# Attention in groups of 128 tokens and all heads, with q, k and the output transposed by DMA, ahead of a SwiGLU block

## The chip, the cores and the metric

The kernel runs on one core of a Trainium2 chip. The metric is the device time of one execution in microseconds (us), as the median of several runs. The profile comes from one of these executions. Its span, from the first to the last instruction, is about 2 us shorter than the run's time.

The engines are PE (matmul), DVE (vector), ACT (scalar functions), POOL (general purpose) and SP (which here only issues DMAs). In the timelines below, each of them works through its own instructions in order (in the change, ACT's first exp, whose scores PE had finished by 11.7 us, stands behind DMA issues and starts at 28.8 us).

## The reference

```python
q, k, v: (8, 8, 576, 64)            # batch, heads, tokens, head_dim
scores = q @ k.T / 8, masked to 0 <= row - column < 64
attn   = softmax(scores) @ v
x      = attn as (4608, 512)        # tokens, heads * head_dim
out    = (silu(x @ w_gate) * (x @ w_val)) @ w_out     # d_ff = 1536
```

Inputs and output are float32. Both kernels compute in bf16 with float32 sums, write silu by way of tanh, and skip the maximum of the softmax.

## The kernel before

A unit is 512 tokens of one pair of heads; there are 36 (9 blocks of 512 tokens, 4 pairs). q and k come in as float32 on partitions of tokens, are cast on POOL and transposed on PE. The keys of a pair are copied into `kbd`, a block-diagonal tile, so that one matmul serves both heads.

```python
def transposes(u):
    q_b, k_b = ready.pop(u)
    tp = ps_a.tile([P, 2, 512], BF16, name="tp", tag="a")
    for i, x in enumerate((q_b, k_b)):
        for c in range(4):
            nc.tensor.transpose(tp[:, i, P * c:P * c + P], x[:, c, :], identb[:])
    qT = att.tile([P, 512], BF16, name="qT", tag="qT")
    nc.scalar.copy(qT[:], tp[:, 0, :])
    kb = kbd[t % 2]
    kt = tp[:, 1, :].rearrange("r (j x) -> r j x", x=64)
    nc.vector.tensor_copy(kb[0:64, p, :, 0:64], kt[0:64])
    nc.vector.tensor_copy(kb[64:128, p, :, 64:128], kt[64:128])
```

The output comes out with channels on partitions, so the softmax sums must be known on every partition. A matmul with a matrix of ones gives them, and DVE takes the reciprocal of a whole 128x512 tile:

```python
def products(u):
    ...
    for c in range(2):
        nc.tensor.matmul(d_ps[:], bones[:], E[:, :, c, :], start=(c == 0), stop=(c == 1))
    nc.vector.reciprocal(r[:], d_ps[:])
    nc.vector.tensor_mul(xT[t][:, p, :], o_ps[:], r[:])
```

A regular round runs one unit of attention ahead of a quarter of the FFN of an earlier block:

```python
gate_value(t, 3 * s)            # 8 matmuls 128x512, tanh on ACT, two DVE operations
products(w + 4)
gate_value(t, 3 * s + 1)
transposes(w + 5)
project(t - 1, s, ps_o, "o")    # 12 matmuls 128x512, copy on ACT, store
load(w + 8); casts(w + 6); scores(w + 5)
gate_value(t, 3 * s + 2)
```

All DMAs go out from SP, some 20 in a round.

The softmax here doesn't subtract the row's maximum and nothing guards it: scores larger than these inputs give would overflow.

Of the kernel before, what the change touches and what calls it, by code (L numbers as in the profile page):

```python
# [17 lines left out]
def kernel(  # L18
# [14 lines left out]

    nc = tc.nc
# [3 lines left out]
    NU = NT * 4  # L38
# [5 lines left out]
    cast = ctx.enter_context(tc.tile_pool(name="cast", bufs=2))  # L44
# [11 lines left out]
    kbd = [cst.tile([P, 4, 8, P], BF16, name=f"kbd{i}") for i in range(2)]  # L56
    vbd = [cst.tile([P, 4, 8, P], BF16, name=f"vbd{i}") for i in range(2)]
    identb = cst.tile([P, P], BF16, name="identb")
    bones = cst.tile([P, P], BF16, name="bones")
    mask = cst.tile([P, 8, 2, 64], BF16, name="mask")  # L60

    def segments(t):

        n0 = 64 * t
        segs = []
        if n0 > 0:
            segs.append((0, t - 1, S - n0, min(n0, 512)))
        if n0 < 512:
            segs.append((n0, t, 0, 512 - n0))
        return segs  # L70

    staged = {}

    def load(u):
        t, p = divmod(u, 4)
        q_f = stage.tile([P, 4, 2, D], FP32, name="q_f", tag="q_f")
        k_f = stage.tile([P, 4, 2, D], FP32, name="k_f", tag="k_f")
        v_f = stage.tile([P, 8, D], FP32, name="v_f", tag="v_f")
        for dst, src in ((q_f, q), (k_f, k)):
            for off, b, s0, n in segments(t):  # L80
                o, s, left = off, s0, n
                while left:
                    if o % P or left < P:
                        m, r = 64, 64
                    else:
                        m, r = left // P * P, P
                    for a in range(2):
                        nc.sync.dma_start(  # L88
                            dst[o % P:o % P + r, o // P:o // P + max(1, m // P), a, :],
                            src[b, 2 * p + a, s:s + m].rearrange("(c r) d -> r c d", r=r),  # L90
                        )
                    o, s, left = o + m, s + m, left - m
        for off, b, s0, n in segments(t):
            for a in range(2):
                nc.sync.dma_start(
                    v_f[64 * a:64 * a + 64, off // 64:(off + n) // 64],
                    v[b, 2 * p + a, s0:s0 + n].rearrange("(j r) d -> r j d", r=64),
                )
        staged[u] = (q_f, k_f, v_f)

    ready = {}

    def casts(u):
        t, p = divmod(u, 4)
        q_f, k_f, v_f = staged.pop(u)
        q_b = cast.tile([P, 4, P], BF16, name="q_b", tag="q_b")
        k_b = cast.tile([P, 4, P], BF16, name="k_b", tag="k_b")
        nc.gpsimd.tensor_copy(q_b[:], q_f[:].rearrange("r c h d -> r c (h d)"))  # L108
        nc.gpsimd.tensor_copy(k_b[:], k_f[:].rearrange("r c h d -> r c (h d)"))  # L109
        vb = vbd[t % 2]  # L110
        nc.gpsimd.tensor_copy(vb[0:64, p, :, 0:64], v_f[0:64])
        nc.gpsimd.tensor_copy(vb[64:128, p, :, 64:128], v_f[64:128])
        ready[u] = (q_b, k_b)
# [3 lines left out]
    def weights_gv(s):  # L117
        for i, src in enumerate((moe_w_gate, moe_w_val)):
            w_f = wst.tile([P, 4, 384], FP32, name="w_f", tag="w_f")
            nc.sync.dma_start(  # L120
                w_f[:], src[:, 384 * s:384 * s + 384].rearrange("(c r) f -> r c f", r=P)
            )
            raw[i, s] = w_f

    def casts_gv(s):
        for i, dst in enumerate((wg, wv)):
            nc.vector.tensor_copy(dst[:, :, 384 * s:384 * s + 384], raw.pop((i, s))[:])

    def weights_o(s):
        w_f = wst.tile([P, 3, DM], FP32, name="wo_f", tag="w_f")  # L130
        nc.sync.dma_start(
            w_f[:], moe_w_out[384 * s:384 * s + 384].rearrange("(c r) f -> r c f", r=P)
        )
        raw[2, s] = w_f

    def casts_o(s):
        nc.vector.tensor_scalar_mul(wo[:, 3 * s:3 * s + 3, :], raw.pop((2, s))[:], 0.5)

    queries = {}

    def transposes(u):
        t, p = divmod(u, 4)
        q_b, k_b = ready.pop(u)
        tp = ps_a.tile([P, 2, 512], BF16, name="tp", tag="a")
        for i, x in enumerate((q_b, k_b)):
            for c in range(4):
                nc.tensor.transpose(tp[:, i, P * c:P * c + P], x[:, c, :], identb[:])  # L147
        qT = att.tile([P, 512], BF16, name="qT", tag="qT")
        nc.scalar.copy(qT[:], tp[:, 0, :])  # L149
        kb = kbd[t % 2]  # L150
        kt = tp[:, 1, :].rearrange("r (j x) -> r j x", x=64)
        nc.vector.tensor_copy(kb[0:64, p, :, 0:64], kt[0:64])  # L152
        nc.vector.tensor_copy(kb[64:128, p, :, 64:128], kt[64:128])  # L153
        queries[u] = qT

    weights = {}

    def scores(u):
        t, p = divmod(u, 4)
        qT = queries.pop(u)  # L160
        E = att.tile([P, 8, 2, 64], BF16, name="E", tag="E")
        Ef = E[:].rearrange("r m c x -> r (m c x)")
        for h in range(2):
            s_ps = ps_a.tile([P, 512], FP32, name="s_ps", tag="a")
            lo = 0
            if u < 4 and h == 0:
                lo = 64
            else:
                j = 4 * h - 1
                kb = kbd[t % 2][:, p, j, :] if j > 0 else kbd[(t - 1) % 2][:, p, 7, :]  # L170
                nc.tensor.matmul(s_ps[:, 0:64], kb, qT[:, 256 * h:256 * h + 64])
            for i in range(4):
                n = P if i < 3 else 64
                j = 4 * h + i
                nc.tensor.matmul(  # L175
                    s_ps[:, 64 + P * i:64 + P * i + n],
                    kbd[t % 2][:, p, j, :],
                    qT[:, 64 * j:64 * j + n],
                )
            nc.scalar.activation(  # L180
                Ef[:, 512 * h + lo:512 * h + 512], s_ps[:, lo:512], AF.Exp, scale=0.125
            )
            nc.gpsimd.tensor_mul(  # L183
                Ef[:, 512 * h + lo:512 * h + 512],
                Ef[:, 512 * h + lo:512 * h + 512],
                mask[:].rearrange("r m c x -> r (m c x)")[:, lo:512],
            )
            if t < 8 and t // 4 == h:
                nc.gpsimd.memset(E[:, t, 0, :], 0.0)
        weights[u] = E  # L190

    xT = {}

    def products(u):
        t, p = divmod(u, 4)
        E = weights.pop(u)
        Ef = E[:].rearrange("r m c x -> r (m c x)")
        if p == 0:
            xT[t] = xpool.tile([P, 4, 512], BF16, name="xT", tag="xT")
        o_ps = ps_a.tile([P, 512], FP32, name="ao_ps", tag="a")  # L200
        first = True
        for j in range(-1, 8):
            if j < 0 and t == 0:
                continue
            vb = vbd[t % 2][:, p, j, :] if j >= 0 else vbd[(t - 1) % 2][:, p, 7, :]
            lo, hi = max(0, 64 * j), min(512, 64 * j + P)
            e0 = 64 * (2 * j + 1) if j >= 0 else 0
            nc.tensor.matmul(
                o_ps[:, lo:hi], vb, Ef[:, e0:e0 + hi - lo],
                start=first, stop=(j == 7), skip_group_check=True,  # L210
            )
            first = False
        d_ps = ps_a.tile([P, 512], FP32, name="ad_ps", tag="a")
        for c in range(2):
            nc.tensor.matmul(d_ps[:], bones[:], E[:, :, c, :], start=(c == 0), stop=(c == 1))  # L215
        r = att.tile([P, 512], FP32, name="r", tag="r")
        nc.vector.reciprocal(r[:], d_ps[:])  # L217
        nc.vector.tensor_mul(xT[t][:, p, :], o_ps[:], r[:])  # L218
# [3 lines left out]
    def gate_value(t, m):  # L222
# [13 lines left out]
        nc.vector.scalar_tensor_tensor(sg[:], th[:], 1.0, g_ps[:], ALU.add, ALU.mult)  # L236
        nc.vector.tensor_mul(hT[t][:, m, :], sg[:], v_ps[:])  # L237

    def project(t, s, pool, tag):
        o_ps = pool.tile([P, 512], FP32, name="o_ps", tag=tag)  # L240
# [6 lines left out]
        nc.scalar.copy(os_[:], o_ps[:])  # L247
        nc.sync.dma_start(out[512 * t + P * s:512 * t + P * s + P, :], os_[:])


    for u in range(4):
        load(u)
    weights_gv(0)
    load(4)
    for i in range(2):
        nc.vector.memset(kbd[i][:], 0.0)
    make_identity(nc, identb[:])
    for i in range(2):
        nc.vector.memset(vbd[i][:], 0.0)
    casts(0)  # L260
# [111 lines left out]
```

## Time and profile before

| | before |
|---|---|
| time, median of 3 | 470.63 us (470.52 to 470.74) |
| span of the profiled execution | 468.9 us |
| regular round | 11.53 us |
| a round without attention (at the end) | 7.77 us |
| first gate matmul | 40.8 us |
| first gate matmul after 24 gate/value steps and 4 projections | 149.8 us |

The last row is read from the timeline of PE. It is there because the two kernels fill their start-up with different amounts of FFN work: at that point both have done the same. The text calls it the milestone, or the start of the regular rounds.

Lines of the page of the kernel before: busy time of each engine with its share of the span; the strips, which cut the span in 40 slices and give the busy tenths of each (9 is 90% or more); the DMA queue; and the chain of waits that ended last, by engine and by line.

```profile
span 468.9 us, 6826 instructions
PE 367.7 (78%) x2332; PEld 189.3 (40%) x2332; DVE 338.8 (72%) x380; ACT 145.2 (31%) x253; POOL 176.9 (38%) x258
...
PE   1453866738888888888888888888888888889996
...
DMA  7965567741332355333333443233343330001012
...
q1 hardware_dynamic: 129280, 47.22, 39.3%
...
DVE 52%; PE 35%; ACT 4%; SPq 3%; issue 2%; POOL 2%; DMA 1%; DVEq 0%; POOLq 0%; ACTq 0%
```

PE has the most busy time, but the chain names DVE first. The groups say why. Their columns are line, engine, operation, tiles, shapes and count, then the busy time, the mean ns of one, and the idle time of the engine just before them with what ended it:

```profile
L217 DVE RECIPROCAL r<-ad_ps 128x512 f32<-128x512 f32 x36 | 120.7, 3353 | 5.0 <-PE ad_ps L215 5.0
...
L175 PE MATMUL s_ps<-qT,kbd_93 128*128 128x128 bf16 (+1 forms) x160 | 14.0, 232 | 33.0 <-DVE kbd_93 L153 31.6
...
L175 PE MATMUL s_ps<-qT,kbd_94 128*128 128x128 bf16 (+1 forms) x128 | 10.3, 224 | 29.2 <-DVE kbd_94 L153 29.2
```

PE stood idle for 61 us in all before the score matmuls, until DVE had copied the keys. The timeline of DVE in one regular round shows what held the copies. Columns are the start, the length, and then the instruction:

```profile
245.14 3.35 DVE L217 RECIPROCAL r<-ad_ps 128x512 f32<-128x512 f32 x1
248.53 0.69 DVE L218 TENSOR_TENSOR xT<-ao_ps,r 128x512 bf16<-128x512 f32 x1
249.13 0.68 DVE L236 SCALAR_TENSOR_TENSOR sg<-th,g_ps 128x512 f32<-128x512 f32 x1
249.91 0.69 DVE L237 TENSOR_TENSOR hT<-sg,v_ps 128x512 bf16<-128x512 f32 x1
250.52 0.41 DVE L152 COPY kbd_94<-tp 64x512 bf16<-64x512 bf16 x1
250.94 0.43 DVE L153 COPY kbd_94<-tp 64x512 bf16<-64x512 bf16 x1
```

The reciprocal of 3.35 us and what queues up behind it stand ahead of the key copies, and PE gets its scores at 251.42 us after a gap of 1.81 us.

### The profile page before, as it was taken

The numbers are of one execution on the slowest core, as the hardware profiler recorded it, in microseconds if no ns is written. First come the engines' busy times: TensorE is split into PE (matmuls) and PEld (weight loads), VectorE is DVE, ScalarE is ACT, GpSimd is POOL, SyncE is SP. The second block draws the span as 40 slices with busy tenths as digits, with TensorE's granted clock in tenths as the row PEclk, the third lists the DMA queues.
The fourth block names the chain that finished last, engine by engine and source line by source line (L and its number), as shares of the span: only waits on it lengthen the run. The fifth ranks groups of instructions, "written<-read, shape, count | busy, mean of one in ns | idle before, by whom it ended". The sixth has DMA issues, their size and how long they took to land.

```text
span 468.9 us, 6826 instructions
## 1 busy us (share of the span) xinstructions
PE 367.7 (78%) x2332; PEld 189.3 (40%) x2332; DVE 338.8 (72%) x380; ACT 145.2 (31%) x253; POOL 176.9 (38%) x258
## 2 busy tenths in 40 slices
PE   1453866738888888888888888888888888889996
PEld 0331433414444444444444444444444444444443
DVE  7188798777777777777777777777777777776540
ACT  1220222313333333333333333333333333323232
POOL 3873445424444444444444444444444433110000
PEclk9975897879999999999999999999999999999999
DMA  7965567741332355333333443233343330001012
GB/s 173 253 182 130 154 183 209 219 104 46 87 87 67 79 138 124 87 76 82 87 86 92 119 111 90 70 90 92 90 113 92 91 89 24 22 24 45 22 46 89
DMA packets 129314, 47.65 MB, mean 102 GB/s; under 512 B 119040, under 2 KB 123136, under 8 KB 129280
## 3 DMA queue, kind: packets, MB, share of 16 engines
q1 hardware_dynamic: 129280, 47.22, 39.3%
q8 instruction: 18, 0.29, 0.3%
q14 instruction: 16, 0.13, 0.1%
HBM read 37.75 MB, written 9.44 MB: 101 GB/s over the span
## 4 chain that ended last, share of the span: by engine, by line
DVE 52%; PE 35%; ACT 4%; SPq 3%; issue 2%; POOL 2%; DMA 1%; DVEq 0%; POOLq 0%; ACTq 0%
DVE r L217 24%; PE g_ps L229 14%; PE v_ps L229 9%; DVE hT L237 9%; DVE sg L236 8%; PE o_ps L242 6%; DVE xT L218 5%; PE s_ps L175 4%; ACT th L234 3%; SPq L88 2%; POOL E L183 2%; DVE kbd_93 L153 1%; DVE kbd_94 L153 1%; DVE kbd_93 L152 1%; PE ad_ps L215 1%
## 5 line engine op out<-in xcount | busy, mean ns | idle before, releaser
L183 POOL TENSOR_TENSOR E<-E,mask 128x512 bf16<-128x512 bf16 (+1 forms) x72 | 84.5, 1185 | 215.4 <-ACT E L180 215.4
L236 DVE SCALAR_TENSOR_TENSOR sg<-th,g_ps 128x512 f32<-128x512 f32 x108 | 73.9, 684 | 86.5 <-ACT th L234 86.4
L217 DVE RECIPROCAL r<-ad_ps 128x512 f32<-128x512 f32 x36 | 120.7, 3353 | 5.0 <-PE ad_ps L215 5.0
L229 PE MATMUL g_ps<-xT,wg 128*128 128x512 bf16 x432 | 115.4, 391 | 2.9 <-DVE xT L218 2.9
L229 PE MATMUL v_ps<-xT,wv 128*128 128x512 bf16 x432 | 114.3, 388 | 0.0
L234 ACT ACTIVATE th<-g_ps 128x512 f32<-128x512 f32 x108 | 64.5, 597 | 128.4 <-PE g_ps L229 128.4
L242 PE MATMUL o_ps<-wo,hT 128*128 128x512 bf16 x432 | 98.6, 379 | 0.0
L237 DVE TENSOR_TENSOR hT<-sg,v_ps 128x512 bf16<-128x512 f32 x108 | 74.2, 687 | 11.6 <-PE v_ps L229 0.6
L229 PEld LDWEIGHTS <-wv 128*128 128x128 bf16 x432 | 43.3, 100 | 57.2 <-issue 8.6
L180 ACT ACTIVATE E<-s_ps 128x512 bf16<-128x512 f32 (+1 forms) x72 | 39.1, 592 | 68.6 <-PE s_ps L175 68.6
L242 PEld LDWEIGHTS <-hT 128*128 128x128 bf16 x432 | 41.1, 98 | 44.6
L229 PEld LDWEIGHTS <-wg 128*128 128x128 bf16 x432 | 40.9, 100 | 44.5 <-issue 3.5
L175 PE MATMUL s_ps<-qT,kbd_93 128*128 128x128 bf16 (+1 forms) x160 | 14.0, 232 | 33.0 <-DVE kbd_93 L153 31.6
L149 ACT COPY qT<-tp 128x512 bf16<-128x512 bf16 x36 | 21.1, 586 | 45.6 <-PE tp L147 45.6
L175 PE MATMUL s_ps<-qT,kbd_94 128*128 128x128 bf16 (+1 forms) x128 | 10.3, 224 | 29.2 <-DVE kbd_94 L153 29.2
L147 PE MATMUL tp<-identb,q_b 128*128 128x128 bf16 x144 | 14.8, 229 | 16.9 <-POOL q_b L108 16.9
L215 PE MATMUL ad_ps<-E,bones 128*128 128x512 bf16 x72 | 23.1, 405 | 5.4 <-DVE r L217 5.4
L175 PEld LDWEIGHTS <-kbd_93 128*128 128x128 bf16 x160 | 10.8, 107 | 39.1 <-DVE kbd_93 L153 36.3
L218 DVE TENSOR_TENSOR xT<-ao_ps,r 128x512 bf16<-128x512 f32 x36 | 24.9, 692 | 1.2
L108 POOL CAST q_b<-q_f 128x512 bf16<-128x512 f32 x36 | 22.7, 630 | 6.1 <-DMA q_f<-in_q_dram 4.5
L109 POOL CAST k_b<-k_f 128x512 bf16<-128x512 f32 x36 | 22.1, 613 | 4.3 <-PE g_ps L229 3.3
L147 PEld LDWEIGHTS <-q_b 128*128 128x128 bf16 x144 | 11.3, 102 | 26.0 <-POOL q_b L108 18.2
(77 smaller groups left out, 240.7 us busy)
## 6 DMA issues: line engine op xcount, KB each, us to landing
w_f<-in_moe_w_gate_dram SPq DMA_DIRECT2D x4, 768.0 KB, 5.4
w_f<-in_moe_w_val_dram SPq DMA_DIRECT2D x4, 768.0 KB, 7.1
q_f<-in_q_dram SPq DMA_DIRECT2D x32, 96.0 KB, 3.8
k_f<-in_k_dram SPq DMA_DIRECT2D x32, 96.0 KB, 2.4
wo_f<-in_moe_w_out_dram SPq DMA_DIRECT2D x4, 768.0 KB, 6.0
q_f<-in_q_dram SPq DMA_DIRECT2D x16, 128.0 KB, 2.8
k_f<-in_k_dram SPq DMA_DIRECT2D x16, 128.0 KB, 3.2
v_f<-in_v_dram SPq DMA_DIRECT2D x16, 128.0 KB, 3.2
```

What stands on the lines that cost most here:

```text
L147: nc.tensor.transpose(tp[:, i, P * c:P * c + P], x[:, c, :], identb[:])
L175: nc.tensor.matmul(s_ps[:, 64 + P * i:64 + P * i + n], kbd[t % 2][:, p, j, :], qT[:, 64 * j:64 * j + n],)
L180: nc.scalar.activation(Ef[:, 512 * h + lo:512 * h + 512], s_ps[:, lo:512], AF.Exp, scale=0.125)
L183: nc.gpsimd.tensor_mul(Ef[:, 512 * h + lo:512 * h + 512], Ef[:, 512 * h + lo:512 * h + 512], mask[:].rearrange("r m c x -> r (m c x)")[:, ...
L215: nc.tensor.matmul(d_ps[:], bones[:], E[:, :, c, :], start=(c == 0), stop=(c == 1))
L217: nc.vector.reciprocal(r[:], d_ps[:])
L218: nc.vector.tensor_mul(xT[t][:, p, :], o_ps[:], r[:])
L229: nc.tensor.matmul(ps[:], w[:, c, P * m:P * m + P], xT[t][:, c, :], start=(c == 0), stop=(c == 3),)
L234: nc.scalar.activation(th[:], g_ps[:], AF.Tanh, scale=0.5)
L236: nc.vector.scalar_tensor_tensor(sg[:], th[:], 1.0, g_ps[:], ALU.add, ALU.mult)
L237: nc.vector.tensor_mul(hT[t][:, m, :], sg[:], v_ps[:])
L242: nc.tensor.matmul(o_ps[:], hT[t][:, c, P * s:P * s + P], wo[:, c, :], start=(c == 0), stop=(c == 11),)
```

## The change

The intent is to take the large reciprocal and the ones-matmuls away. A unit becomes a group of 128 tokens and all 8 heads. The products are turned round: the tokens are on the output's partitions, the values get two columns of ones (130 columns wide), so that the sums come out of the same matmul as one number per token and head, and the reciprocal has 4 columns. The price is that `x` now has tokens on its partitions and must be transposed for the FFN. That transpose and those of q and k go to DMA, so that PE and the PSUM copies are free of them. q, k and the weights are loaded by few large DMAs issued on ACT; v, the stores and the transposes are issued on SP. The start-up interleaves the first two blocks of 512 tokens.

The core of the diff (the loads, score layout, start-up order and lines within these pieces are cut):

```diff
-        for i, x in enumerate((q_b, k_b)):
-            for c in range(4):
-                nc.tensor.transpose(tp[:, i, P * c:P * c + P], x[:, c, :], identb[:])
-        nc.scalar.copy(qT[:], tp[:, 0, :])
+    def turn(g):
+        sp.dma_start_transpose(out=kT[:], in_=k_b[:])
+        sp.dma_start_transpose(out=qT[:, g % QR], in_=q_b[:])
+    def spread(g):
+        for a in range(2):
+            dve.tensor_copy(
+                kb[64 * a:64 * a + 64, :, :, 64 * a:64 * a + 64],
+                kT[64 * a:64 * a + 64].rearrange("r p (i x) -> r p i x", i=2),
+            )
...
-        for c in range(2):
-            nc.tensor.matmul(d_ps[:], bones[:], E[:, :, c, :], start=(c == 0), stop=(c == 1))
-        nc.vector.reciprocal(r[:], d_ps[:])
-        nc.vector.tensor_mul(xT[t][:, p, :], o_ps[:], r[:])
+            dve.reciprocal(r[:], o_ps[:, :, P:VW])          # 128x4
+            dve.tensor_mul(x_b[...], o_ps[:, :, 0:P]..., r[:]...)
+        sp.dma_start_transpose(out=xT[t][:, :, P * s:P * s + P], in_=x_b[:])
...
+    for w in range(8, NG):
+        turn(w + 6)
+        gate_value(t, 3 * s)
+        products(w + 4)
+        spread(w + 6)
+        casts(w + 7, pool)
+        gate_value(t, 3 * s + 1)
+        scores(w + 6, pool)
+        casts_v(w + 6)
+        load_v(w + 8, sp)
+        load_qk(w + 9, act)
+        project(t - 1, s, ps_o, "o")
+        gate_value(t, 3 * s + 2)
```

## The prediction

> **What bounds it now.** Three stages, read from the chain of waits and the timeline.
> (a) To about 103 us: start-up. The 40-slice strip shows DMA engines 50-90% busy at 130-250 GB/s and PE mostly half idle. Only the 12 gate/value steps of the first 512 tokens get done.
> (b) 103 to 414 us: 27 equal rounds of 11.53 us, each a quarter of 512 tokens. The chain alternates DVE (52%) and PE (35%). In each round DVE's reciprocal (128x512, 3.35 us, 121 us in all) holds back the kbd copies behind it; PE waits 1.8-2.0 us for them before the scores (61 us under "PE s_ps <- DVE kbd" in the waits). PE's own work in a round: FFN 7.77 us (read off the last rounds, which have no attention and repeat every 7.77 us) plus attention, about 1.8 us.
> (c) From 422 us: four rounds of pure FFN and a last projection (10.4 us), PE-bound.
> SP is near its limit too: some 20 DMA issues per round at about 0.55 us each, 11 of 11.5 us.
>
> **Removed.** The big reciprocal: 36 x 3.35 us becomes 72 of 4 columns, about 0.1 us each (estimate from 6.5 ns per column). PE transposes (36 x 8 x 128 columns) and the ones-matmuls for the sums (36 x 2 x 512): 74k columns, 31 us of PE at the traced 0.86 us per 4x512. ACT's qT copy (21 us). kbd copies from PSUM (30 us), replaced by copies from SBUF.
> **Added.** Products stream 3x130 columns per pair: 56k instead of 37k, +8 us PE. PE attention per 128 tokens: 20 matmuls at about 57 ns (traced spacing of the 128-column ones) = 1.15 us. [...] 108 DMA transposes of 128 KB on SP. [...]
> **Moved.** q/k/weight loads to ACT's queue (2-4 issues, 1-2 us per round; ACT then about 5.5 us). Start-up order: 512-token blocks 0 and 1 are interleaved, so PE has 24 gate/value steps and 4 projections to run while weights arrive.
>
> **Sum.** Steady rounds become PE-bound: 7.77 + 1.15 = 8.9, say 9.0 us. First gate at about 40 us, as now (same bytes to load). From there to the regular rounds: 41.5 (24 steps) + 10.4 (projections) + 11 (attention of ten groups) plus some cold clock and waits: they start at about 110 us, with 31 us more FFN done than now at 103. Then 24 x 9.0 = 216, 4 x 7.77 = 31, end 10.4 + 3.5. Span about 371-377; time 378 us, range 355 to 430. Gain: about 60 us from rounds, about 30 from start-up.
>
> Chances: faster 0.88, same 0.05, slower 0.07.
>
> **Signs.** Right if the chain is mostly PE in the middle, with PE 90% busy or more at a period of 8.9-9.3 us; DVE about 60-65%; no reciprocal among the costly groups; the chain names DMA transposes only in start-up. Start-up right if the first gate matmul comes near 40 us and the first projection near 100 us.
>
> **What would make it wrong.** SP occupied over about 2 us per transpose: then SP sets the period (3T + 2.7 us; T = 3 gives 11.7 us, no gain). The same if transposes stall ordinary DMA traffic, or if DVE waits for kT. In start-up, transposes compete with saturated loads, and each group needs three in series; the first gate could slip to 60 us. ACT's in-order DMA issues might delay tanh.

DVE's copies from SBUF (the "spread") had no traced copy behind them, and the sign "DVE about 60-65%" rested on that estimate. The forecast's sum loses no term: it came to a span of about 371 to 377 us and a time of 378 us, range 355 to 430. That SP and DVE keep below PE's 9.0 us in a round, which the sum takes for granted, was an estimate. "Cold clock" in it is the granted clock in the trace of the kernel before: 0.88 in the first 40 us, 0.80 from 40 to 103 us, 1.00 in the rounds. ACT's 5.5 us fit six traced operations of about 0.6 us and the 1 to 2 us of issues.

## The result, and the profile after

The changed kernel takes 452.9 us (451.52 to 453.13, 3 runs) against 470.63 us. The ratio is 0.9615, with a 95% interval of 0.9585 to 0.9645. It is faster, by a fifth of what was predicted (17.7 us against 93), and outside the predicted range. Ratios here are the mean time of one kernel's fast runs over that of the other's fast runs in the same rounds, so they are not quite the ratio of the medians.

The same lines of the page, of the kernel after:

```profile
span 451.1 us, 6021 instructions
PE 347.6 (77%) x2032; PEld 174.5 (39%) x2032; DVE 230.7 (51%) x482; ACT 126.0 (28%) x219; POOL 151.6 (34%) x221
...
PE   0014363755767676999999999999899999999996
...
DMA  9999569965493359678987778976868842110012
...
q1 hardware_dynamic: 103104, 33.06, 38.7%
q10 hardware_dynamic: 80832, 28.32, 29.1%
...
PE 43%; DMA 22%; DVE 17%; POOL 5%; ACT 4%; issue 4%; SPq 2%; ACTq 1%; DVEq 0%; POOLq 0%
```

DVE lost 108 us of work. PE is at 9 in the middle slices where it was at 8. But the first 16 slices (180 us) are poor, with PE mostly at 3 to 7, and DMA is now 22% of the chain. The queues' share of the DMA engines has risen from 39% to 68%. The groups that replace the reciprocal, and the copies of the keys:

```profile
L216 DVE RECIPROCAL r<-ao_ps 128x4 f32<-128x4 f32 x72 | 12.5, 174 | 4.6 <-PE ao_ps L212 4.4
L217 DVE TENSOR_TENSOR x_b<-ao_ps,r 128x256 bf16<-128x256 f32 x72 | 30.5, 424 | 2.5
```

The reciprocals cost 12.5 us where they cost 120.7. In a regular round PE has one small gap left. From the timelines of PE and DVE:

```profile
257.48 0.22 PE L175 MATMUL s_ps<-qT,kbd_93 128*128 128x128 bf16 x1
258.17 0.23 PE L181 MATMUL s_ps<-qT,kbd_94 128*128 128x128 bf16 x1 [0.47 <-DVE kbd_94 L132]
```

```profile
257.19 0.42 DVE L217 TENSOR_TENSOR x_b<-ao_ps,r 128x256 bf16<-128x256 f32 x1
257.54 0.58 DVE L132 COPY kbd_94<-kT 64x512 bf16<-64x512 bf16 x2
```

The key copies follow the normalisation in DVE's order, and here only that order makes them wait: the transposed k had landed at 256.25 us. In 6 of the 22 regular rounds, though, they began within 0.2 us of k's landing, so there the landing was what held them. The period is 9.54 us instead of the 9.0 that was predicted.

Two milestones on PE's timeline divide the time:

| | before | after | predicted |
|---|---|---|---|
| first gate matmul | 40.8 us | 57.6 us | 40 us |
| first gate matmul after 24 gate/value steps and 4 projections | 149.8 us | 173.5 us | 110 us |
| from there to the end of the span | 319.1 us | 277.6 us | 261 us |

So the regular rounds gained 41.5 us and the start-up gave 23.7 us of it back. By this milestone it had been expected to gain 40. The question for the experiments is therefore what holds the start-up.

The waits of the changed kernel in the first 182 us (the line that waited, what it waited for, us in all, how often, the longest):

```profile
PE s_ps L181 <- DVE kbd_94 L132: 21.2, 3, 15.4
PE s_ps L175 <- DMA qT<-q_b: 20.3, 8, 3.9
...
ACT L185 <- DMA v_f<-in_v_dram: 27.5, 1, 27.5
...
ACT th L239 <- DMA kT<-k_b: 19.7, 3, 7.2
...
PE g_ps L234 <- DVE sg L241: 11.8, 3, 4.2
```

Two kinds of wait stand out. PE waits for the transposed q, and for the copies of transposed k. And ACT, which needs no DMA'd data for exp or tanh, waits for DMAs: its first exp came at 28.8 us, although PE had finished that group's score matmuls by 11.7 us. The packed trace and the program's instruction list, which is built from the kernel and is no view of the profile, explain that. In the trace, the 380 DMAs issued from SP and ACT signal eight completion semaphores, 47 or 48 DMAs each; in the list the eight come in turn over both engines. None of the 372 issues that use a semaphore again began before the earlier DMA with this semaphore had landed; the closest came 0.02 us after it. Of ACT's 19 such issues in the first 60 us, 13 began within 0.1 us of that landing. On ACT, exp and tanh stand behind such issues:

```
10 L142 DMACopy w_f<-in_moe_w_val_dram 128x4x384 [waits DMAHW5_49]
11 L86 DMACopy k_f<-in_k_dram 64x8x64 [waits DMAHW0_49,DVE_49]
...
16 L185 Activation E_102<-s_ps 128x2x128 [waits PE_49] x2
```

The durations of the transposes themselves can be read off: SP is occupied for 1.2 to 1.25 us by one of 128x512. From issue to landing, in the issues view, the medians in the stretch 200 to 400 us are these (the last column):

```profile
xT<-x_b SPq DMA_TRANSPOSE x21, 2.4
kT<-k_b SPq DMA_TRANSPOSE x19, 3.5
qT<-q_b SPq DMA_TRANSPOSE x19, 2.5
```

The shortest of the 108 needed 2.4 us until it had landed. In the first 60 us the medians are 4.1 (k), 3.2 (q) and 4.1 us (x). One transpose of x, issued at 89.2 us behind two weight loads of 768 KB (84.3 and 84.7 us) and a load each of k and q (88.6 and 89.0 us), took 6.9 us to land, and the gate matmuls that need it started at 96.1 us, after 5.1 us of idle PE.

Landing is only a part of what delays the keys. SP sends its DMAs in order, and the next k stands behind the transpose of x:

```profile
40.36 1.23 SPq L223 DMA_TRANSPOSE xT<-x_b  x1
41.64 1.26 SPq L124 DMA_TRANSPOSE kT<-k_b  x1
```

This k had been cast by 34.7 us and landed at 45.3 us: 6.9 us before the issue and 3.7 us from there to landing. Of the 14 groups of the start-up, 6 had their keys copied within 0.4 us of k's landing; for the other 8 the copies began 3.7 to 17 us after it, behind other work in DVE's order.

### The profile page after: what moved, and what is told of

Its sections match the earlier page's. It is cut to its first block, busy times and chain, and to the rows that moved or that the text cites. A ratio compares the mean times of both kernels' runs of the same rounds, so it can differ in the third digit from the quotient of the medians.

```text
span 451.1 us, 6021 instructions
## 1 busy us (share of the span) xinstructions
PE 347.6 (77%) x2032; PEld 174.5 (39%) x2032; DVE 230.7 (51%) x482; ACT 126.0 (28%) x219; POOL 151.6 (34%) x221
## 4 chain that ended last, share of the span: by engine, by line
PE 43%; DMA 22%; DVE 17%; POOL 5%; ACT 4%; issue 4%; SPq 2%; ACTq 1%; DVEq 0%; POOLq 0%
PE o_ps L247 16%; PE g_ps L234 14%; PE v_ps L234 9%; DMA qT<-q_b 8%; DMA v_f<-in_v_dram 5%; DMA kT<-k_b 5%; DVE sg L241 4%; DVE x_b L217 4%; DVE hT L242 3%; ACT th L239 3%; PE s_ps L181 2%; DMA q_f<-in_q_dram 2%; POOL E_103 L186 1%; PE s_ps L175 1%; POOL k_b L106 1%
## 5 line engine op out<-in xcount | busy, mean ns | idle before, releaser
L234 PE MATMUL g_ps<-xT,wg 128*128 128x512 bf16 x432 | 117.6, 397 | 23.9 <-DVE sg L241 11.8
L234 PE MATMUL v_ps<-xT,wv 128*128 128x512 bf16 x432 | 116.1, 393 | 0.0
L186 POOL TENSOR_TENSOR E_103<-E_103,mask 128x512 bf16<-128x512 bf16 x14 | 15.8, 1152 | 49.2 <-ACT E_103 L185 49.2
L217 DVE TENSOR_TENSOR x_b<-ao_ps,r 128x256 bf16<-128x256 f32 x72 | 30.5, 424 | 2.5
L186 POOL TENSOR_TENSOR E_105<-E_105,mask 128x512 bf16<-128x512 bf16 x14 | 15.9, 1152 | 43.7 <-ACT E_105 L185 43.7
L186 POOL TENSOR_TENSOR E_104<-E_104,mask 128x512 bf16<-128x512 bf16 x14 | 15.8, 1153 | 43.0 <-ACT E_104 L185 43.0
L186 POOL TENSOR_TENSOR E_102<-E_102,mask 128x512 bf16<-128x512 bf16 (+1 forms) x14 | 14.4, 1049 | 42.3 <-ACT E_102 L185 42.3
L181 PE MATMUL s_ps<-qT,kbd_94 128*128 128x128 bf16 x48 | 7.9, 243 | 23.9 <-DVE kbd_94 L132 23.9
L106 POOL CAST k_b<-k_f 128x512 bf16<-128x512 f32 x28 | 17.8, 635 | 21.3 <-DMA kT<-k_b 12.1
L181 PE MATMUL s_ps<-qT,kbd_93 128*128 128x128 bf16 x48 | 7.2, 236 | 18.1 <-DMA qT<-q_b 11.1
L108 POOL CAST q_b<-q_f 128x512 bf16<-128x512 f32 x28 | 17.8, 635 | 4.5 <-DMA q_f<-in_q_dram 3.1
L175 PE MATMUL s_ps<-qT,kbd_93 128*128 128x128 bf16 x48 | 8.8, 240 | 10.9 <-DMA qT<-q_b 10.9
L175 PE MATMUL s_ps<-qT,kbd_94 128*128 128x128 bf16 x48 | 8.8, 242 | 10.3 <-DMA qT<-q_b 10.3
L181 PEld LDWEIGHTS <-kbd_94 128*128 128x128 bf16 x48 | 4.9, 108 | 29.7 <-DVE kbd_94 L132 29.6
L216 DVE RECIPROCAL r<-ao_ps 128x4 f32<-128x4 f32 x72 | 12.5, 174 | 4.6 <-PE ao_ps L212 4.4
```

The source lines that it names most:

```text
L106: eng.tensor_copy(k_b[:], k_f[:].rearrange("r h d -> r (h d)"))
L108: eng.tensor_copy(q_b[:], q_f[:].rearrange("r h d -> r (h d)"))
L175: nc.tensor.matmul(s_ps[:, i, 0:4:3, :], kb, x)
L181: nc.tensor.matmul(s_ps[:, i, 1:3, :], kbd[g % KR][:, p, 0, :], qT[:, g % QR, p, :])
L186: eng.tensor_mul(e, e, mask[:, lo:hi, :].unsqueeze(1).to_broadcast([P, 2, hi - lo, 64]))
L216: dve.reciprocal(r[:], o_ps[:, :, P:VW])
```

## The experiments

The theories at the outset, for the start-up:

- A: the loads issued on ACT hold up exp and tanh.
- B: the DMA transposes, by one of three ways: B1, their landing latency in the chain cast, transpose, key copy, scores, products, transpose of x; B2, the DMA engines' time that they take from the loads; B3, their issue time on SP and their turns of the completion semaphores.
- C: the bytes of the weights simply keep the DMA engines busy.

And for the rounds, D: the order of the key copies on DVE.

All runs but one gave the reference's result. "Fourth projection" is the time of its copy on ACT: in the changed kernel 172.1 us, where the first tanh comes at 59.5 us. The expectations take the copy of the next projection, 184 us in the changed kernel, for the start of the regular rounds. Their letters differ from the list above: in e1, e2, e5 and e7, B is that the DMA engines are saturated (here B2 and C), and C the transposes in series (here B1). Of the 16 runs, 9 fell outside every range expected for them (e2, e4, e5, both e6, e9, e12, e13 and e15); the sizes below are what was measured, and no confirmed forecasts.

| run | time, us | ratio to before | first tanh | 4th projection | most rounds |
|---|---|---|---|---|---|
| before | 470.6 to 471.8 | 1 | 45.8 | 145.8 | 11.53 |
| the change | 452.9 | 0.9615 | 59.5 | 172.1 | 9.54 |
| e1_loads_on_sp | 457.65 | 0.9727 | 63.6 | 160.3 | 9.5 to 12.0 |
| e2_pe_turn | 474.52 | 1.0074 | 50.4 | 165.9 | 10.84 |
| e4_spread_first | 466.37 | 0.9907 | 57.0 | 170.6 | 8.9 to 12.8 |
| e5_loads_on_pool | 481.85 | 1.0239 | 65.4 | 157.4 | 10 to 13.5 |
| e6_start_on_sp | 448.31 | 0.9496 | 64.1 | 158.6 | 9.54 |
| e6_start_on_pool | 446.95 | 0.9490 | 67.5 | 162.8 | 9.54 |
| e7_less_weights (wrong result) | 443.35 | 0.9409 | 57.0 | 160.7 | 9.54 |
| e9_turn_early | 449.22 | 0.9516 | 57.7 | 169.7 | 8.95, some 10.45 |
| e10_both_fixes | 438.74 | 0.9303 | 64.5 | 161.0 | 8.95 |
| e12_pe_turn_start_sp | 410.98 | 0.8709 | 50.2 | 139.1 | 8.95 |
| e13_pe_turn_start_act | 417.94 | 0.8895 | 54.8 | 149.2 | 8.95 |
| e14_idle_transposes | 430.07 | 0.9123 | 64.4 | 155.7 | 8.95 |
| e15_idle_transposes_act | 428.02 | 0.9085 | 61.3 | 155.7 | 8.95 |
| e16_start_act_steady | 444.03 | 0.9426 | 59.7 | 173.8 | 8.95 |
| e17_small_dmas_on_sp | 428.84 | 0.9092 | 64.1 | 154.7 | 8.95 |
| e18_small_dmas_act | 427.75 | 0.9076 | 60.6 | 154.6 | 8.95 |

The runs with rounds of 8.95 us also have one now and then of 10.2 to 10.9 us. Each profile is of one run, and that of e13 is of its slowest (423.79 us; the other three took 417.6 to 418.1), so that the marks of e13 in this table are late for its median.

### e1, e5: the loads of q, k and weights away from ACT

```diff
-        load_qk(g, act)      # this, and all other loads of q, k and weights
+        load_qk(g, sp)       # e1;  e5: pool
```

> The changed kernel with every q, k and weight load issued from SP's queue instead of ACT's; nothing else. Theory A (ACT held hostage: a load issue on ACT waits until the DMA issued eight places earlier has landed, and exp and tanh stand behind it in ACT's order): no ACT gap ends on a DMA any more, the first gate matmul moves from 57.6 to about 48 us, the regular rounds begin at about 160 us instead of 184, time about 430 us. SP carries about 7.5 us per 9.5 us round and holds, so the regular round stays at 9.54 us. Theory B (the DMA engines are saturated in start-up): no change, 450 to 456 us. Theory C (three transposes in series per group set the pace): the same or slower, since transposes now queue behind loads on SP, 450 to 470 us.

> The changed kernel with every q, k and weight load issued from POOL's queue, [...]SP and ACT then share their eight with fewer DMAs, and no exp or tanh stands behind a load. Theory A: start-up gets shorter by as much as in the run with loads on SP or more (rounds begin at 140 to 165 us), time 410 to 432 us, unless POOL's casts and masks, now behind the loads, become the new wait. Theory B: no change, 450 to 456 us. Theory C: little change, 445 to 455 us.

Measured: 457.65 us (ratio 0.9694 to 0.976) and 481.85 us (1.0172 to 1.0306), both slower than the change. The start-up did get shorter: the fourth projection came 12 and 15 us earlier, although the first tanh came later. But the rounds lost their regularity, 9.5 to 12.0 us with SP's issues and 10 to 13.5 us, one of them 15.6 us, with POOL's. Moving everything is a miss as a repair, but it says that A is real in the start-up, and that ACT's issues are harmless, even needed, in the rounds.

### e6: only the loads ahead of the loop away from ACT

```diff
-    load_qk(5, act)          # the 22 calls ahead of the loop only
+    load_qk(5, sp)           # e6_start_on_sp;  e6_start_on_pool: pool
```

> As the run with all loads on SP, but only the loads of the start-up (everything ahead of the regular rounds) go to SP; the regular rounds issue theirs from ACT as in the changed kernel. Theory A as measured so far (waiting load issues in front of tanh cost 12 to 16 us of start-up, and moving the loads cost the regular rounds because SP then did too much): fourth projection copied out at about 160 us instead of 172, regular rounds 9.5 us as in the changed kernel, time 440 to 446 us. If the loss of the run with all loads on SP came from something else than SP's work in the rounds: 450 us or more.

> The same with POOL in place of SP. Theory A: fourth projection copied out at about 157 us, rounds 9.5 us, time 437 to 444 us.

Measured: 448.31 and 446.95 us, with rounds of 9.54 us as in the change. The fourth projection came 13.5 us earlier from SP and 9.3 us from POOL, yet the total fell only by 4.6 and 6 us, because the first regular round then waited (19.7 us to the next projection, instead of 12.2). A costs something, but far less than the 63 us that are missing.

### e2: q and k transposed on PE in all groups

```diff
-        sp.dma_start_transpose(out=kT[:], in_=k_b[:])
-        sp.dma_start_transpose(out=qT[:, g % QR], in_=q_b[:])
+        tp = ps_a.tile([P, 2, 4, P], BF16, name="tp", tag="a")
+        for i, x in enumerate((k_b, q_b)):
+            for c in range(4):
+                nc.tensor.transpose(tp[:, i, c, :], x[:, P * c:P * c + P], identb[:])
+        dve.tensor_copy(kT[:], tp[:, 0])
+        act.copy(qT[:, g % QR], tp[:, 1])
```

> The changed kernel with q and k turned by PE (8 transposes into one PSUM bank, a DVE and an ACT copy out) instead of by DMA; the attention output is still turned by DMA and loads stay on ACT. Theory C (transpose latency, 2.5 to 6 us each in start-up, is the loss): regular rounds begin at about 140 us instead of 184, time about 415 us. Theory A: part of the gain only, since ACT still waits for landings of v and q/k loads: rounds begin at 165 to 180 us, time 435 to 450 us. PE pays 0.46 us and DVE and ACT 0.6 us more per round.

(The 0.46 and 0.6 us are estimates that fit the trace before: eight transposes on PE at a spacing of 57 ns, and the copy of qT on ACT, 586 ns.)

Measured: 474.52 us (1.0047 to 1.0101). The first tanh came 9 us earlier, but the fourth projection only 6 us, and the rounds took 10.84 us. The waits show why: PE, in order, stood at the transposes for 17 us until POOL had cast k, and 47 us at the scores until DVE had made two copies of k in a row. This experiment put the transposes at the wrong place in PE's order and paid for it in every round. It could not decide about B.

### e4, e9: the key copies ahead of the normalisation

```diff
-        products(w + 4)
         spread(w + 6)
+        products(w + 4)
```

> The changed kernel with the kbd copies put ahead of the products in the regular rounds (one pair of lines swapped). My reading of the regular round (9.54 us against 8.9 of PE work) is that PE stands 0.5 to 0.6 us before the scores because the kbd copies wait on DVE behind the normalisation: then the round falls to about 9.0 us, 24 rounds give 12 to 14 us, time about 439 us. Rival: the landing of the key transpose is what the kbd copies wait for, and then they would block DVE earlier: no gain or a loss, 450 to 460 us. Start-up must be unchanged (first regular round at 184 us).

e9 also issues the transposes of a group a round earlier (the conditions at the ends of the loop are left out):

```diff
-        turn(w + 6)
         gate_value(t, 3 * s)
-        products(w + 4)
-        spread(w + 6)
         casts(w + 7, pool)
+        turn(w + 7)
+        spread(w + 6)
+        products(w + 4)
```

> Spread ahead of products as in the run before, and in the regular rounds the key and query transposes are issued a round earlier, right after their casts, while SP waits for the products. If the loss of the run with spread first came from the keys and queries landing too late (DVE waited 14 us for kT, PE 16 us for qT between 200 and 400 us), the rounds go to 8.9 to 9.1 us: time 438 to 443 us. If the transposes slow down because the DMA engines are at their limit at that pace (0.81 busy at 9.54 us), the rounds stay at 9.5 us or more and the time at 450 us or more.

Measured: e4 466.37 us, worse than the change; e9 449.22 us, better. In e4 PE's wait for DVE's key copies in the stretch 200 to 400 us went away (7 us in the change), and a wait for the transposed q took its place:

```profile
PE s_ps L175 <- DMA qT<-q_b: 15.6, 12, 3.2
```

The copies now stood in DVE's order before k had landed, and the DVE work behind them was late. In the same stretch DVE stood 14.2 us at the copies until k had landed. So the order on DVE was what made the gap (D), but it also hid the landing of the transposes. With the issue a round earlier the rounds fall to 8.95 us, PE-bound, as predicted for the change. Most of the rest of e9's gain was lost to a round of 10.45 us about every fourth time, where the transpose of x landed behind loads of q and k.

### e7: fewer bytes of weights

```diff
-                w_f[:], src[:, 384 * s:384 * s + 384].rearrange("(c r) f -> r c f", r=P)
+                w_f[:, 0], src[0:P, 384 * s:384 * s + 384]     # and the cast repeats these rows
```

The result is wrong: the weights' bytes fall from 9.4 to 2.6 MB.

> Wrong result on purpose: each weight load moves only its first 128 rows (a quarter or a third of the bytes; the cast spreads them over the tile), so 2.5 MB instead of 9.4 MB come in during start-up, with the same number of DMAs and the same order. Theory B (DMA engines saturated in start-up, and transposes land late because bulk loads are in front of them): first gate matmul at 48 us or earlier instead of 57.6, landings of transposes in start-up near 2.5 us, fourth projection copied out at 145 us or earlier instead of 172, time 425 us or less. Theory A alone: the waits in front of tanh get shorter only a little; 440 us or more.

Measured: 443.35 us (two runs; 0.9368 to 0.9449), 9.6 us less than the change, with the first tanh only 2.5 us earlier. That is what 6.8 of the 9.4 MB were worth here (C), and a version that computes the right thing can't have it.

### e10, e12, e13: both repairs, then the start-up's transposes on PE

e10 joins e6_start_on_sp and e9, and moves the loop's loads of q and k behind the third gate step. e12 adds that the groups 0 to 13, those of the start-up, are turned on PE, with the key copies straight from PSUM into `kbd` and the transposes of groups 9 to 11 one gate step ahead of the scores. e13 is e12 with the start-up's loads on ACT.

```diff
-        turn(0)                  # groups 0 to 13, each followed later by spread(g)
+        turn_pe(0)
...
+    def turn_pe(g):
+        k_b, q_b = cast_qk.pop(g)
+        tp = ps_a.tile([P, 2, 4, P], BF16, name="tp", tag="a")
+        for i, x in enumerate((k_b, q_b)):
+            for c in range(4):
+                nc.tensor.transpose(tp[:, i, c, :], x[:, P * c:P * c + P], identb[:])
+        kb = kbd[g % KR]
+        for a in range(2):
+            dve.tensor_copy(
+                kb[64 * a:64 * a + 64, :, :, 64 * a:64 * a + 64],
+                tp[64 * a:64 * a + 64, 0].rearrange("r p (i x) -> r p i x", i=2),
+            )
+        act.copy(qT[:, g % QR], tp[:, 1])
```

> Start-up loads on SP plus the regular rounds with spread first and transposes a round early; in addition the q/k loads of a round are issued after its last gate step, so that the output transpose is not behind them (every fourth round was 10.45 us because its output transpose landed 5 us late). If the two gains add: fourth projection copied out at 158 to 162 us, rounds 8.95 us with the 10.45 us ones gone, time 434 to 441 us.

> As the run with both fixes, and q and k of the start-up (groups 0 to 13) turned by PE straight into the padded key tiles, so 28 of the 42 start-up DMA transposes go. If the rest of the start-up loss is the DMA engines' time for the transposes and their landings behind bulk loads (144 us of DMA-engine work lie in the first 180 us): first gate at 45 to 50 us, fourth projection copied out at 130 to 145 us, time 415 to 428 us. If start-up is held by the order of work on PE, DVE and POOL instead: fourth projection still at 155 us or later, time 432 us or more.

> The same with the start-up loads left on ACT. The difference to the run before is what load issues in front of exp and tanh cost once transposes are out of the way. Theory A: 8 to 15 us slower than with loads on SP. If the ACT waits were only waits for transposes: within 3 us of it.

Measured: 438.74 (0.9269 to 0.9337), 410.98 (0.8681 to 0.8737) and 417.94 us (0.8834 to 0.8956). Turning the first groups on PE is worth 27.8 us, and the loads on ACT cost 7.0 us beside it (8.8 us by the ratios, since one run of e13 was 6 us slower than its others). PE's share of the span in e12:

```profile
PE 349.5 (85%) x2144; PEld 181.8 (44%) x2144; DVE 235.3 (57%) x482; ACT 133.8 (33%) x233; POOL 154.0 (38%) x223
```

e12 beats both kernels: 13% below before and 9% below the change. B is thereby the largest part that these runs found, and what remains is by which of its three ways.

### e14, e17: transposes that nothing waits for, and small DMAs in their place

In e14 the groups 0 to 13 are turned on PE as in e12, and SP issues 28 DMA transposes besides, of a constant tile into tiles that nobody reads. e17 replaces each of them by two DMAs of 64 bytes.

```diff
         act.copy(qT[:, g % QR], tp[:, 1])
+        for i in range(2):
+            sp.dma_start_transpose(out=dump[(2 * g + i) % 8][:], in_=spare[:])     # e14
+            for j in range(2):                                                      # e17
+                sp.dma_start(dump[(4 * g + 2 * i + j) % 8][0:1, 0, 0:32], spare[0:1, 0:32])
```

> The version with the start-up's turning on PE (411.0 us, ratio 0.871), but for each of the groups 0 to 13 SP still issues two 128x512 DMA transposes, of a constant tile into tiles that nothing reads. So the 28 transposes of the start-up still take SP's time and the DMA engines' time, and nothing waits for them to land. Theory 1 (their cost is DMA-engine and queue time taken from the loads): most of the 28 us that the PE version gained comes back, 427 to 438 us, and the first tanh slips from 50 towards 60 us. Theory 2 (their cost is the landing latency in the chain cast, transpose, spread copy, scores): 411 to 416 us, ratio 0.870 to 0.882, the first tanh within 3 us of 50. In between (416 to 427) both count, and the share is read off.

> The version with loads on SP and PE turning (411.0 us, ratio 0.871), each idle transpose replaced by two DMAs of 64 bytes on SP that nothing reads: about the same issue time on SP (estimate 2 x 0.55 us for 1.25), next to no DMA-engine time. If SP's issue time made the 19 us that the idle transposes cost there (430.1), most of it is here as well: 424 to 432 us. If it was the DMA engines' time, 411 to 416 us.

Measured: 430.07 us (0.9084 to 0.9161) and 428.84 us (0.9056 to 0.9128). Of the 27.8 us, 19 are back though nothing waits for the landing. At first sight that speaks for B2. But the small DMAs, which move nothing worth the name, cost the same. The stretches view of the first 60 us, of e12, e14 and e17 in that order, begins with the stretch and its length, PE's busy time (matmuls) and PE's weight loads; the last number but one is the DMA engines' busy share:

```profile
0.00:60.00 60.00, 27.46 (x208) 19.28 (x208) 32.03 (x79) 13.55 (x25) 20.96 (x49) 1.00 0.89 180
```

```profile
0.00:60.00 60.00, 17.53 (x144) 13.73 (x144) 25.09 (x61) 10.81 (x20) 19.15 (x46) 0.90 0.91 175
```

```profile
0.00:60.00 60.00, 18.31 (x144) 14.26 (x144) 24.64 (x62) 10.89 (x20) 19.86 (x46) 1.00 0.73 150
```

In e17 the engines had room to spare, and PE got as little done (18.3 us against 27.5 in e12) as in e14. So B2 is unlikely in this set-up. It isn't excluded: the 56 small DMAs take twice as many turns of the semaphores as the 28 transposes, and could owe to these turns what the transposes owe to the engines' time. B3 shows in SP's timeline, where the second pair of weight loads goes out, in the same order, e12, e14, e17:

```profile
32.54 0.61 SPq L158 DMA_DIRECT2D w_f<-in_moe_w_gate_dram  x1
```

```profile
11.90 3.04 SPq L146 DMA_TRANSPOSE dump<-spare  x2
...
43.11 0.61 SPq L162 DMA_DIRECT2D w_f<-in_moe_w_gate_dram  x1
```

```profile
11.78 2.97 SPq L147 DMA_DIRECT2D dump<-spare  x4
...
42.38 0.61 SPq L163 DMA_DIRECT2D w_f<-in_moe_w_gate_dram  x1
```

SP was busy back to back; two transposes or four small DMAs took 2.5 to 3.7 us of it each time, and the weights went out 10 us later.

### e15, e16, e18: the same with the loads on ACT, as the change has them

e16 is the change with nothing but e10's order of the rounds. e15 is e13 with the idle transposes, e18 is e13 with the small DMAs. These four, e16, e15, e18 and e13, differ only in how the start-up's q and k are turned and in what SP issues besides.

> The change as it is, start-up untouched (DMA transposes for all groups, loads on ACT), with only the new order of the regular rounds. It is the reference for the idle transposes with the loads on ACT: the same start-up traffic, but waited for. Rounds 8.95 us as in the runs with that order, start-up as in the change (4th projection at about 170 us): 440 to 449 us. If waiting for the landings costs nothing beyond the traffic, the idle version comes out at the same time; if the landings' latency is what costs, this one is 15 us or more above the idle one.

> The same idle transposes (28 of 128x512 that nothing waits for) in the version that turns on PE and keeps the q, k and weight loads on ACT (417.9 us, ratio 0.890), as the change itself has them. SP then issues only the v loads, the stores and the transposes, so it is far from full, and the loads of q, k and weights can't be held up in its order. If the transposes cost mainly by SP's issue time (in the run before, SP was busy back to back and the second pair of weight loads was issued 10.6 us later), little is lost here: 418 to 423 us, ratio up to 0.90. If they cost by the DMA engines' time, which they take wherever they are issued, it is 430 to 437 us, ratio 0.915 to 0.93, as in the run with the loads on SP.

> The small DMAs on SP (56 of 64 bytes, about the issue time of the 28 transposes) in the version that turns on PE with the loads on ACT (417.9 us, ratio 0.890; with idle transposes 428.0, ratio 0.909). If the 10 us of the idle transposes there are SP's issue time and the turns of the completion semaphores, they are here as well: 426 to 430 us. If they are the DMA engines' time (the small DMAs take next to none), 417 to 420 us.

Measured: e16 444.03 us (0.9385 to 0.9467), e15 428.02 us (0.9052 to 0.9118; in neither of its ranges), e18 427.75 us (0.9052 to 0.91), e13 417.94 us. So in the change's own set-up the DMA transposes of q and k cost 26.1 us in the start-up. 16.0 us of that go when nothing waits for their landing (B1). With them go the waits that led PE's list in the first 160 us of e16 (in e15 the longest is 14.2 us, for ACT's exp):

```profile
PE s_ps L181 <- DVE kbd L132: 37.5, 8, 13.9
PE s_ps L175 <- DMA qT<-q_b: 17.1, 6, 4.2
```

PE then does the turning itself, DVE copies the keys from PSUM, and k no longer stands behind the transpose of x in SP's order, so this is the worth of the whole exchange; how much of it is landing alone was not tested. The other 10.1 us (8.9 by the ratios) stay with idle transposes and equally with small DMAs (B3), so the DMA engines' time (B2) isn't seen here either, with the same reservation about the turns. How B3 reaches the loads on ACT can be read from ACT's timeline, e13 first and e18 second: the load of the fifth k and the first exp.

```profile
17.47 1.41 ACTq L88 DMA_DIRECT2D k_f<-in_k_dram  x2
...
22.88 0.66 ACT L201 ACTIVATE E<-s_ps 128x256 bf16<-128x256 f32 x2 [6.04 <-issue]
```

```profile
22.98 1.38 ACTq L90 DMA_DIRECT2D k_f<-in_k_dram  x2
...
26.80 0.66 ACT L206 ACTIVATE E<-s_ps 128x256 bf16<-128x256 f32 x2 [14.06 <-DMA k_f<-in_k_dram]
```

In both programs this load waits for nothing but its completion semaphore, by the instruction list:

```
14 L90 DMACopy k_f<-in_k_dram 64x8x64 [waits DMAHW2_49]
```

With more DMAs in the common turn of the eight semaphores it went out 5.5 us later, and the exp behind it came 3.9 us later (in the slowest run of e13, as said). From 34 us on SP was nearly back to back in e18 as well. How much of the 10 us is the semaphores' turn and how much SP's time is not told apart.

## Why the prediction was wrong

**Right: what is removed.** The reciprocal went from 120.7 to 12.5 us, DVE from 338.8 to 230.7 us busy, PE lost 20 us of work, and the chain turned from DVE to PE. A transpose occupies SP for 1.2 us, below the 2 us above which SP would have set the period by the forecast, and lands after 2.4 to 3.5 us in the rounds.

**Nearly right: the rounds.** Predicted 9.0 us, measured 9.54; from the milestone to the end 277.6 us instead of 261 us. PE's own work was counted rightly, as the 8.95 us rounds of e9 and e16 show. What was missed is that the key copies stand behind the normalisation in DVE's order. The new order took the change from 452.9 to 444.0 us (e16).

**The step that failed: "they start at about 110 us".** The sum for it was a first gate matmul "at about 40 us, as now (same bytes to load)", then PE's work of 41.5 + 10.4 + 11 us "plus some cold clock and waits". Measured: first gate at 57.6 us, regular rounds at 173.5 us. The miss of 63.5 us at the milestone makes up most of the 80 us by which the span missed 371 us, the lower end of the predicted span, which is the sum of those terms; the rounds make up the other 16.6 us. The stretch from the first gate on was priced by PE's work, about 63 to 70 us, and took 116 us, of which PE was busy 75 us. So it was not PE's work that was mis-sized above all, but the waits between, which the sum left out: in this stretch PE stood some 21 us for the transposed q and the copies of k, 12 us for DVE's gate operations and 9 us for the transposed x. Each group's keys and queries have to be cast, issued, landed and copied in the orders of SP, ACT and DVE. The prediction's reason for "as now" was the bytes; the bytes were not what decided, as e7 shows (9.6 us for 6.8 MB of 9.4).

What the runs put in its place, as steps from the change to the best version; the sizes hold for this order of steps and these set-ups:

| step | runs | us |
|---|---|---|
| key copies and transposes earlier in the rounds, loads of q and k later (D) | the change to e16 | 8.9 |
| PE turns q and k in the start-up: nothing waits for a DMA transpose of them to be issued and to land (B1) | e16 to e15 | 16.0 |
| those transposes aren't issued (B3) | e15 to e13 | 10.1 |
| the start-up's loads off ACT (A) | e13 to e12 | 7.0 |
| sum | 452.9 to 411.0 | 41.9 |

With the start-up's loads on SP the split is another: B1 8.7 us (e10 to e14), B3 19.1 us (e14 to e12). And A is worth 5.3 us beside DMA transposes (e16 to e10), but costs 2.1 us beside idle ones (e15 to e14), which SP has to send as well. With all steps the start-up ends at 138.9 us instead of 173.5, which is 35 of the 63.5 us missed. The first gate, which had been put at 40 us, comes at 57.8 us in e16, 59.4 in e15, 52.8 in e13 and 48.3 us in e12: B1 did nothing for it.

The prediction named three of these as risks: that transposes compete in the start-up and the first gate "could slip to 60 us", that "ACT's in-order DMA issues might delay tanh", and three transposes in series per group. It then gave the sum almost nothing for them, and its range ended below the result. It also had the competition in another place than the one that e14 to e18 point to: not the DMA engines' time, but the issuing engines' and the turns of the semaphores. Fewer, larger DMAs had lowered the number of issues (528 in the trace before, 380 after), but each transpose of q and k is an issue with a waiter behind it.

**Open.** e12's regular rounds start at 138.9 us, still 29 us after the predicted 110. Its waits in that stretch have many causes, among them a transpose of x that took 6.9 us to land and held the gate matmuls for 7.6 us. PE's clock is part of it as well: four gate matmuls in a row took 1.87 us at 80.6 us, right after that idle stretch, and 1.03 us from 84.3 us on, as in the rounds. The clock records of e12 show a granted share of 0.5 from 76.9 to 83.7 us and 1.0 after it (the mean from 60 to 100 us is 0.91), but no run here was made to price it. Nor was the transpose of x moved to PE.

## What to carry to other kernels

A stage at the start where data is late is not priced by the work of the busiest engine: follow one group through it, with each issue, landing and copy in series, and count what the issuing engines must send in that time. A DMA that waits for its turn belongs in the order of an engine that has nothing urgent behind it and not too much to send: SP's in the start-up of e12 (411.0 us, against 417.9 with ACT's, e13), but not with 56 small DMAs more (428.8 us, e17), nor in the rounds of e1 (9.5 to 12.0 us, against 9.54). A DMA transpose that is free in the rounds, issued a round ahead (8.95 us a round in e16, which is PE's own work), can hold up everything behind it in the start-up (26.1 us from e16 to e13), where PE has time to do it (it was busy for 27.5 of the first 60 us in e12).
